# Second layer of the second block of 336 slots: 20 products over 3 x 4 tiles in the next block's steps, sums of its weights on GpSimd

## The chip, the cores and the metric

One core of one Trainium2 chip. The metric is the device time of one execution in microseconds; all numbers below are microseconds unless marked ns. The engines are TensorE (PE; PEld is its weight load), VectorE (DVE), ScalarE (ACT), GpSimd (POOL) and SyncE (SP, which only issues DMAs here).

## The reference

An RWKV-5 attention (4 batches, 8 heads, 768 tokens, 48 per head) gives 3072 tokens of D = 384. They go through a mixture of 8 experts with one expert per token:

```python
for b in range(B):
    for s in range(S):
        # e: the token's own argmax, or the token before's expert, by a gate
        h = np.maximum(x[b, s] @ w1[e], 0.0)     # 384 -> 1024
        out[b, s] = p[e] * (h @ w2[e])           # 1024 -> 384
```

Everything is float32. What follows is about the two layers `x @ w1[e]` and `h @ w2[e]` of the experts.

## The kernel before

Attention and routing take the first 107 us or so. Then the experts' tokens are worked through in ten *units*, each a number of slots of one expert: two early ones of 168, then `BLOCKS` of 448, 424, 392, 376, 336, 336, 256 and 192. Counted from 0 they are units 2 to 9; the change is about **unit 7**, the second one of 336. Its neighbours are unit 6 (336), unit 8 (256) and unit 9 (192), the last.

*First layer of units 2 to 8* (`twenty`, L1227). A product of 3 D tiles x 4 F tiles x 2 token halves is made with 20 products instead of 24, for each half `g` of F. It has 10 steps (`STEPS`), and a unit so has 20, two halves of ten. A step writes its two matmuls into one of two PSUM banks (`lanes`; steps 0 to 9 use banks 0, 1, 1, 0, 1, 1, 0, 1, 0, 1), ACT copies the bank to `snap` (L1270), DVE joins what belongs together into `hg` (L1254), ACT applies the relu in place (L1259, L1262). The factors are sums of weights (`weight_sums`, 16 DVE instructions of 128x256, L1224) and of tokens (`token_sums`, 14 instructions on the unit's half width, L1210), made while the unit before is worked on.

*Second layer* (`seven`, L1324). The first 256 slots of a unit are multiplied as pairs of 2 x 2 blocks with seven products instead of eight: four pairs, 28 matmuls of 128x192, whose factors DVE makes (`sums` L1293, `factors` L1302). What is over 256 slots (80 for a unit of 336) takes plain matmuls (`rest`, L1334: 8 of 128x384). DVE joins the seven banks (L1394), ACT scales by the gate (L1412), POOL scatters the rows to the output (L1417).

*The order.* It is written by hand. After each step of a first layer `twenty` calls `wide(i, g, s)`, which gives out a little of everything else: matmuls of the second layer by the table `BEHIND` (its first half, F tiles 0 to 3, in the own unit's steps of g = 1, its second half in the next unit's steps of g = 0), and so many DVE steps from the lists `ws`, `ts`, `fs`, `js` by the tuples in the code. These fills lie between a step's matmuls and the next ones, while ACT copies the bank. POOL gathers the tokens of the unit after the next one (L1159), each gather behind a copy of one column to `seen` (L1155), which holds it until `hg` has come so far. SP fetches weights in the order in which buffers come free (`fetch`).

*The end.* Unit 9 is done plainly in a final loop over its 8 F tiles (`hidden` L1186, then `rows` L1427 and `half_rows` L1434); unit 8's second half of the second layer lies in it by the table `LAST`. The last rows are scaled on DVE (L1444) and scattered.

Each engine works through its own queue in order.

Of the kernel before, what the change touches and what calls it, by code (L numbers as in the profile page):

```python
# [20 lines left out]
P = 128  # L21
# [1048 lines left out]
class Experts:  # L1070
# [6 lines left out]

    def __init__(self, tc, st, x_d, w1, w2, out, ident, router):
# [11 lines left out]
        self.units += [unit(None, n, b * ST, r.gid, r.sid, r.gate) for b, n in enumerate(BLOCKS)]  # L1090

        self.outs = dram_disjoint_views(out, sum(len(u["cols"]) for u in self.units))
# [121 lines left out]
    def weight_sums(self, i):  # L1214

        nc, u = self.nc, self.units[i]
        w, t = u["w1"], self.weps[i % 2].tile([P, 14, 2, P], F32, name="ws", tag="ws")
        u["ws"] = t

        def of(a):  # L1220
            return t[:, a] if isinstance(a, int) else w[:, a[0]::4, a[1]]

        def step(out, a, b, op):
            return lambda: nc.vector.tensor_tensor(t[:, out], of(a), of(b), op=Alu.add if op == "+" else Alu.subtract)  # L1224

        return [step(*s) for s in WEIGHT_SUMS]

# [6 lines left out]
    def twenty(self, i, g, then):  # L1234
# [29 lines left out]
        for s, (c, k, place) in enumerate(STEPS):  # L1264
            bank = self.lanes[min(c, 1)]
            for z, (a, b) in enumerate(CHAINS[c][k]):
                nc.tensor.matmul(bank[:, z * n:(z + 1) * n], lhsT=left(a), rhs=right(b), start=(k == 0 and z == 0),  # L1267
                                 stop=(k == len(CHAINS[c]) - 1), skip_group_check=True)
            source = bank[:, :2 * n].rearrange("p (x c) -> p x c", x=2)
            nc.scalar.copy(self.snap[:, place, :, :n], source[:, ::-1] if (c, k) in TURNED else source)  # L1270
            self.settle()
            self.owed[0].extend(join(*j) for j in JOINS.get(s, ()))
            if s in DONE:
                self.owed[1].append(lambda s=s: done(DONE[s]))
            then(s)

    def output(self, i, m, tiles=range(DK)):
# [176 lines left out]
    def send(self, i, j):  # L1454
        nc, u = self.nc, self.units[i]
        n, c = u["rows"][j], u["cols"][j]
        tp = self.bank("otp")[:, :D].rearrange("p (k t) -> p k t", k=DK)
        first = j * P - (2 * P if u["seven"] else 0)
        for d in range(DK):
            nc.tensor.transpose(tp[:n, d], u["yT"][:, d, first:first + n], self.ident)  # L1460
        yo = self.op.tile([P, D], F32, name="yo", tag="yo")
# [56 lines left out]
    def run(self, att, flag, ready, free):  # L1518
# [10 lines left out]
        self.router.powers(0)  # L1529
        behind, fs, ws, ts, js, ends = {}, [], [], [], [], []  # L1530

# [17 lines left out]
        def joined(k):  # L1549
# [16 lines left out]
        def wide(i, g, s):  # L1566
# [4 lines left out]
            early = k < EARLY  # L1571
            if s == 0:
# [3 lines left out]
            if s in (1, 2) and not early:  # L1576
                self.sums(k, 2 * z + s - 1)
            at = g * 10 + s - (6 if i == EARLY else 1)
            if (i, g, s) == (EARLY, 0, 2):
# [8 lines left out]
            elif (g, s) in ((0, 9), (1, 1), (1, 3), (1, 5), (1, 7), (1, 9)) and (i, g, s) > (EARLY, 1, 2):  # L1588
                sent()
            fill(*BEHIND[s])  # L1590
            if not u["rest"] and (g, s) in ((1, 0), (1, 1)):
                self.hidden(i + 1, s, self.tp[1])
            if g == 0:
                if s == 0 and not early:
                    fs.extend(self.factors(k, 3))
                if s == (6 if i == EARLY else 3):
# [4 lines left out]
                some(ws, (0, 0, 0, 0, 0, 0, 0, 0, 0, 2)[s] if i == EARLY else (0, 0, 0, 0, 0, 3, 4, 3, 3, 0)[s])  # L1601
                if i == EARLY and s == 4:
                    drained(k)
                    self.fetch(i + 1, self.nc.sync, 2)
                if s == 9 and not early:
                    joined(k)
# [3 lines left out]
            else:  # L1610
# [18 lines left out]
        for i in range(n):  # L1629
# [11 lines left out]

            lag = 6 if i == n - 1 else 1
            for m in range(FK):
                if following and m == FK - 1:
                    turned(i + 1, after - 1)
                if i < n - 1 or m > 1:
                    self.hidden(i, m)
                if (i, m) == (0, 0):
                    att.turn(B * HP - 1, yb[1:])
                if i == n - 1:  # L1650
                    if m in (2, 3, 4):
                        self.settle()
                    if m == 2:
                        behind = self.seven(i - 1, 1)
                        fs.extend(self.factors(i - 1, 3))
                        some(fs, 4)
                    if m in (2, 3):
                        self.sums(i - 1, m)
                    if m in LAST:
                        fill(*LAST[m])  # L1660
                    if m == 5:
                        joined(i - 1)
                        some(js, 9)
                    if m in (6, 7):
                        some(ends, 1)
                if sends and m >= 1 and i > EARLY:
                    self.send(*sends.pop(0))
                if i == n - 1:
                    if m >= lag:
                        self.rows(m - lag)  # L1670
                elif m >= lag and not (following and m > FK - 3):
                    self.output(i, m - lag)
# [6 lines left out]
                if following and m == 3:  # L1679
                    ws.extend(self.weight_sums(i + 1))  # L1680
                if following and m >= 3:
# [11 lines left out]
        for m in range(FK - lag, FK):  # L1693
            self.rows(m)
        self.send_rows(0)
        self.half_rows()
# [46 lines left out]
def kernel(  # L1743
# [41 lines left out]
    with ExitStack() as st, tc.manual_schedule():  # L1785
        ro = st.enter_context(tc.tile_pool(name="ro", bufs=1))
        mpp = st.enter_context(tc.tile_pool(name="mpp", bufs=1, space=PSUM))
        router = Router(tc, ro, mpp, lt, mask, ident, gid, sid, gate, over[:, 0:1])
        ex = Experts(tc, st, x_d, w1, w2, out, ident, router)
        att = Attention(tc, st, rk_d, kv_d, vT_d, x_d, w_t, wp_d, kept, ident, lt, router.mp)  # L1790
# [100 lines left out]
```

## Time and profile before

| | us |
|---|---|
| median of 3 runs | 367.23 (366.93 to 367.93) |
| the profiled execution | 367.12 |
| its span, first to last instruction | 365.4 |
| SP's weight fetches, 1536 KB each, w1: issue to landing | 6.7 |
| sums of tokens, 128x168 on DVE (L1210), mean | 0.326 |

A group of the profile has the line, engine and operation, the tiles written and read, the shape and the count, then its busy time and the mean ns of one, then the engine's idle time ahead of it and what ended it. In a list by time the columns are the start from the span's first instruction, the busy time, the engine, line and operation, and how many instructions lie in that row. A 128x192 matmul of float32 is two records, and a row's count counts records.

### The profile page before, as it was taken

Reading aid. Unit: us, or ns where it says so; the run is one execution under the profiler, and the core shown is the slowest. Engines: PE = TensorE matmul, PEld = TensorE weight load, DVE = VectorE, ACT = ScalarE, POOL = GpSimd, SP = SyncE. Lnnn points to the kernel's source line nnn. Section 1 sums busy time; section 2 is a strip of 40 time slices with the busy share of each in tenths; the row PEclk is TensorE's granted clock in tenths of the full one; section 3 lists DMA queues with packets and bytes.
Section 4 is the critical chain, followed back from the end, with each engine's and each line's share of the span. In section 5 each row is a group of like instructions: output and inputs, shape, how many; then the busy total and the mean of one; then the engine's idle time right before and its main releaser. Section 6 shows DMA issues by size and latency. Waiting matters only on the chain. (4 is left out here: it accounts for less than half of the span.)

```text
span 365.4 us, 9346 instructions
## 1 busy us (share of the span) xinstructions
PE 355.2 (97%) x3574; PEld 309.9 (85%) x3574; DVE 281.6 (77%) x806; ACT 158.2 (43%) x397; POOL 167.1 (46%) x212
## 2 busy tenths in 40 slices
PE   7999999999999999999999999999999999999991
PEld 4776877777769999888889999998998988899971
DVE  7888778788835768897989869879979989947530
ACT  5222232223523214845545557546555546546310
POOL 8589999789522057128174115313604114012022
PEclk9999999999999999999999999999999999999997
DMA  7999999992658766914125516416336326425011
GB/s 252 410 408 408 407 409 380 356 348 101 215 175 292 277 224 215 395 60 162 68 101 192 194 35 226 155 61 237 97 135 236 132 86 228 173 68 198 2 44 37
DMA packets 17380, 74.91 MB, mean 205 GB/s; under 512 B 2394, under 2 KB 6240, under 8 KB 15024
## 3 DMA queue, kind: packets, MB, share of 16 engines
q1 hardware_dynamic: 10336, 56.89, 41.6%
q0 software_dynamic: 3424, 9.48, 7.6%
q10 hardware_dynamic: 3568, 7.87, 5.8%
q8 instruction: 30, 0.49, 0.5%
q14 instruction: 22, 0.18, 0.2%
HBM read 64.79 MB, written 9.47 MB: 203 GB/s over the span
## 5 line engine op out<-in xcount | busy, mean ns | idle before, releaser
L1270 ACT COPY snap<-h 128x336 f32<-128x336 f32 (+5 forms) x140 | 65.0, 464 | 88.1 <-PE h L1267 83.4
L1417 POOL DMA_INDIRECT out_dram<-yo,sid x27 | 32.4, 1201 | 92.7 <-ACT yo L1412 77.1
L1159 POOL DMA_INDIRECT xg<-x_d,gid x29 | 32.8, 1131 | 28.6 <-DVE gid L926 19.3
L1267 PE MATMUL h<-xs,ws 128*128 128x168 f32 (+5 forms) x224 | 44.2, 320 | 0.0
L1254 DVE TENSOR_TENSOR hg<-snap 128x336 f32<-128x336 f32 (+5 forms) x56 | 30.0, 536 | 18.2 <-ACT snap L1270 17.8
L1267 PEld LDWEIGHTS h<-xs,ws 128*128 128x128 f32 x224 | 37.2, 190 | 5.2 <-issue 1.4
L1324 PE MATMUL y<-factors,sums 128*128 128x192 f32 x168 | 38.8, 327 | 0.0
L326 DVE TENSOR_TENSOR am<-pair,kept 128x768 f32<-128x768 f32 x32 | 29.9, 952 | 9.3 <-PE pair L316 5.7
L1155 POOL COPY seen<-hg 128x1 f32<-128x1 f32 x26 | 12.5, 480 | 52.0 <-ACT hg L1259 47.6
L240 POOL TENSOR_TENSOR pd<-rk 128x384 f32<-128x384 f32 x32 | 31.8, 1016 | 7.4 <-DMA rk<-in_rk_dram 3.9
L1324 PEld LDWEIGHTS y<-factors,sums 128*128 128x128 f32 x168 | 28.4, 190 | 0.1
L1324 PE MATMUL y<-w2t,hg 128*128 128x192 f32 x112 | 25.3, 328 | 0.0
L1334 PE MATMUL tp<-w2t,hg 128*80 128x384 f32 (+2 forms) x64 | 24.6, 487 | 0.0
L354 ACT COPY xT<-y 128x768 f32<-128x768 f32 x15 | 12.0, 798 | 29.0 <-PE y L346 29.0
L1224 DVE TENSOR_TENSOR ws<-w1t 128x256 f32<-128x256 f32 x56 | 21.9, 416 | 3.3 <-DMA w1t<-in_w_dram 3.3
L257 POOL TENSOR_TENSOR rw<-rk,tab 128x384 f32<-128x384 f32 x26 | 23.6, 932 | 0.4 <-DMA rk<-in_rk_dram 0.4
L1186 PE MATMUL h<-exT,w1t 128*128 128x168 f32 (+1 forms) x132 | 23.5, 315 | 0.0
L333 PE MATMUL y<-am,kv 128*64 128x128 f32 x360 | 23.0, 277 | 0.0
L236 POOL TENSOR_TENSOR ke<-kv,endT 128x288 f32<-128x288 f32 (+1 forms) x32 | 21.9, 706 | 0.9 <-DMA kv<-in_kv_dram 0.9
L1267 PE MATMUL h<-exT,ws 128*128 128x168 f32 (+5 forms) x112 | 22.1, 319 | 0.0
L1267 PE MATMUL h<-xs,w1t 128*128 128x168 f32 (+5 forms) x112 | 21.8, 319 | 0.0
L333 PEld LDWEIGHTS y<-am,kv 128*64 128x64 f32 x360 | 19.3, 137 | 1.9 <-issue 1.1
(296 smaller groups left out, 799.4 us busy)
## 6 DMA issues: line engine op xcount, KB each, us to landing
w1t<-in_w_dram SPq DMA_DIRECT2D x8, 1536.0 KB, 6.7
w2t<-in_w_dram SPq DMA_DIRECT2D x8, 1536.0 KB
rk<-in_rk_dram SPq DMA_DIRECT2D x15, 768.0 KB, 8.7
kv<-in_kv_dram SPq DMA_DIRECT2D x16, 584.0 KB, 8.1
vT<-in_vT_dram SPq DMA_DIRECT2D x16, 384.0 KB
x_d<-x ACTq DMA_DIRECT2D x4, 1152.0 KB
w1t<-in_w_dram SPq DMA_DIRECT2D x2, 768.0 KB
w2t<-in_w_dram SPq DMA_DIRECT2D x2, 768.0 KB
```

Source lines behind the costliest of these rows:

```text
L240: nc.gpsimd.tensor_mul(t["pd"][:, z], t["rT"][:, z], t["kT"][:, z])
L257: engine.tensor_mul(t["rw"][:, z], t["rT"][:, z], spread(pw, 1, z.stop - z.start))
L326: return lambda: nc.vector.tensor_mul(t["am"][:, g], sc, spread(kept, 1, 2))
L333: nc.tensor.matmul(t["y"][h][p * DP:(p + 1) * DP, c2 * P:(c2 + 1) * P], lhsT=t["v"][:, (2 * c + h) * DH:(2 * c + h) * DH + DP], rhs=t["am" ...
L1159: self.nc.gpsimd.indirect_dma_start(out=xg[:n], out_offset=None, in_=self.x_d[:rows], in_offset=bass.IndirectOffsetOnAxis(ap=u["gid"][:n, ...
L1186: nc.tensor.matmul(h[:, :n], lhsT=u["w1"][:, m, kk, :], rhs=u["xT"][:, kk, :], start=(kk == 0), stop=(kk == DK - 1))
L1254: return lambda: nc.vector.tensor_tensor(o, a, self.snap[:, b, :, :n], op=Alu.add if op == "+" else Alu.subtract)
L1267: nc.tensor.matmul(bank[:, z * n:(z + 1) * n], lhsT=left(a), rhs=right(b), start=(k == 0 and z == 0), stop=(k == len(CHAINS[c]) - 1), skip ...
L1270: nc.scalar.copy(self.snap[:, place, :, :n], source[:, ::-1] if (c, k) in TURNED else source)
L1324: nc.tensor.matmul(bank[:, x * half:(x + 1) * half], lhsT=a(), rhs=b(), start=first, stop=(count(k) == FK // 2), skip_group_check=True)
L1334: nc.tensor.matmul(u["y"][:z, :D], lhsT=u[m][:, 2 * P:2 * P + z], rhs=h[:, m], start=first, stop=last)
L1417: self.nc.gpsimd.indirect_dma_start(out=out.rearrange("n (h d) -> (n h) d", h=2) if half else out, out_offset=bass.IndirectOffsetOnAxis(ap ...
```

## The change

Unit 7's second layer no longer goes through `seven`. It is computed transposed, as the first layer is: 3 D tiles x 4 F tiles x 2 token halves (168 slots each) in 20 products for each half of F, 40 matmuls of 128x168 (`deeply`). They lie in unit 8's 20 steps, by the table `DEEP`. Their weight factors are 16 sums of 128x256 (`second_sums`), made on POOL; their token factors are sums of halves of `hg` on DVE (`halves`); ACT copies six banks (`keep`), DVE joins them (`side`). The result comes out transposed, so that nine transposes and three scalings follow in the final loop (`send`).

Eight of the sixteen weight sums of unit 8's first layer (`ASIDE`) go to POOL as well. Unit 6's second half of the second layer is spread over all of unit 7's 20 steps (`LONG`) and joined at the end of unit 7 instead of its middle; unit 8's second layer lies wholly in the final loop (`LAST`), as do all of unit 9's matmuls. Nothing before unit 6's second half changes.

```diff
+SECOND_SUMS = ((1, (0, 0), (0, 2), "+"), (0, (1, 1), (1, 0), "-"), (2, 0, (2, 1), "-"), (3, (2, 2), 1, "-"),
...
+DEEP = (((), ((16, 0), (17, 0)), ()),
+        (("S1",), ((16, 1), (17, 1)), ("u",)),
...
+        (("y1",), (), ()))
+LONG = (("r2",), ("1b", "r0"), ("r1",), ("1a",), ("2a", "r3"), ("6a",), ("7a",), (), ("3a",), (),
+        ("4a", "5a"), ("2b", "6b"), (), (), ("7b", "3b"), (), ("4b",), ("5b", "hr"), (), ())
+ASIDE = (10, 11, 4, 5, 12, 13, 14, 15)
...
+        if i != self.deep + 1:
+            return [step(nc.vector, *s) for s in WEIGHT_SUMS], []
+        return ([step(nc.vector, *WEIGHT_SUMS[k]) for k in range(16) if k not in ASIDE],
+                [step(nc.gpsimd, *WEIGHT_SUMS[k]) for k in ASIDE])
...
+    def second_sums(self, i, homes):
...
+            return t[a] if isinstance(a, int) else u["w2"][:, a[0]::4, a[1] * P:(a[1] + 1) * P]
+        def step(out, a, b, op):
+            return lambda: nc.gpsimd.tensor_tensor(t[out], of(a), of(b), op=Alu.add if op == "+" else Alu.subtract)
+        return [step(*s) for s in SECOND_SUMS]
...
+        def halves(k, g):
...
+                    nc.vector.tensor_tensor(out, of(a, g), of(b, g), op=add if op == "+" else sub)
+        def product(k, g):
...
+            c, z, a, b = PRODUCTS[k]
+            w = u["ss"][a][:, g] if isinstance(a, int) else u["w2"][:, 4 * g + a[0], a[1] * P:(a[1] + 1) * P]
+            nc.tensor.matmul(banks[c][:, z * n:(z + 1) * n], lhsT=w, rhs=of(b, g), start=c not in begun, stop=False,
+                             skip_group_check=True)
...
+            nc.scalar.copy(t, part(c)[:, ::-1] if k == "u" else part(c))
...
+            if deep:
+                some(ss, 1)
+                if at == 16:
+                    steps.append(self.deeply(i))
+                if at > 17:
+                    steps[0]((("S0", "V0")[at - 18:at - 17], (), ()))
+            if i == self.deep - 1 and at > 14:
+                if at == 15:
+                    ss.extend(self.second_sums(i + 1, homes))
+                some(ss, 2)
+            if done:
+                steps[0](DEEP[at])
...
+            fill(*(LONG[g * 10 + s] if deep else BEHIND[s]))
...
                 if s == 5 and following:
-                    ws.extend(self.weight_sums(i + 1))
+                    steps1, more = self.weight_sums(i + 1)
+                    ws.extend(steps1)
+                    ss.extend(more)
```

The order on POOL from unit 6's second half to the gathers of unit 9's tokens. Before, three scatters (L1417) stand in a row, two of them in unit 6's second half and the third late in unit 7's first, and behind them the gathers (L1155, L1159):

```order
L1155 COPY seen<-hg 128x1
L1159 DMA xg<-x_d,gid 128x384
L1417 DMA out_dram<-yo,sid 3072x384 x3
L1155 COPY seen<-hg 128x1
L1159 DMA xg<-x_d,gid 128x384
L1155 COPY seen<-hg 128x1
L1159 DMA xg<-x_d,gid 64x384
```

After, two scatters (L1582) are followed by eight sums (L1344, `ss`, of unit 7's second weights `w2t`), and then by these rows, in which `ws` are the sums of unit 8's first weights `w1t` (L1274):

```order
L1344 TENSOR_TENSOR ss<-w2t,ss 128x256
L1344 TENSOR_TENSOR ss<-ss,w2t 128x256
L1344 TENSOR_TENSOR ss<-w2t 128x256 x2
L1344 TENSOR_TENSOR ss<-ss 128x256 x2
L1344 TENSOR_TENSOR ss<-w2t,ss 128x256
L1582 DMA out_dram<-yo,sid 3072x384
L1344 TENSOR_TENSOR ss<-w2t,ss 128x256
L1274 TENSOR_TENSOR ws<-w1t 128x256 x2
L1274 TENSOR_TENSOR ws<-ws,w1t 128x256
L1201 COPY seen<-hg 128x1
L1205 DMA xg<-x_d,gid 128x384
L1274 TENSOR_TENSOR ws<-ws,w1t 128x256
```

The 16 sums `ss` and the first three of the eight `ws` now stand ahead of the first gather of unit 9's tokens.

The order on TensorE in unit 7's second half, from the second step on (L1320 is the first layer's line after, L1267 before; L1489 and L1324 the products of `seven`). Before, with unit 7's own products and rest (L1334) as fills:

```order
L1267 MATMUL h<-xs,ws 128x168 x2
L1324 MATMUL y_3747<-w2t,hg 128x192
L1334 MATMUL tp_1790<-w2t,hg 80x384 x2
L1267 MATMUL h<-exT,ws 128x168 x2
L1324 MATMUL y_3747<-w2t,hg 128x192 x2
L1267 MATMUL h<-xs,ws 128x168 x2
L1324 MATMUL y_3749<-factors,sums 128x192 x2
L1267 MATMUL h<-exT,ws 128x168 x2
```

After, with what is left of unit 6's second half:

```order
L1320 MATMUL h<-xs,ws 128x168 x2
L1489 MATMUL y_3503<-w2t,hg 128x192
L1489 MATMUL y_3505<-factors,sums 128x192
L1320 MATMUL h<-exT,ws 128x168 x2
L1320 MATMUL h<-xs,ws 128x168 x2
L1320 MATMUL h<-exT,ws 128x168 x2
L1489 MATMUL y_3505<-factors,sums 128x192
L1489 MATMUL mp<-w2t,sums 128x192
```

Steps 1 and 2, which use the same bank, have two products of 192 between them, and steps 2 and 4 only step 3; the plain matmuls of 384 are gone.

The order on DVE at the start of unit 8. Before, from the second join (L1254) of unit 8's first layer on, `factors` are those of unit 7's `seven`, and L1394 are its joins:

```order
L1254 TENSOR_TENSOR hg<-hg,snap 128x256
L1302 TENSOR_TENSOR factors<-factors,w2t 128x192
L1254 TENSOR_TENSOR hg<-snap 128x2x128
L1254 TENSOR_TENSOR hg<-hg,snap 128x2x128
L1254 TENSOR_TENSOR hg<-snap 128x256
L1394 TENSOR_TENSOR yo<-y_3747,t 128x192
L1394 TENSOR_TENSOR t<-y_3749,t 128x192 x2
```

After, the tile named `factors` (and `xs` further on) holds the sums of halves of unit 7's `hg` (L1385, L1387), and L1408 is a join of `deeply`:

```order
L1307 TENSOR_TENSOR hg<-snap 128x256
L1307 TENSOR_TENSOR hg<-hg,snap 128x256
L1387 TENSOR_TENSOR factors<-factors,hg 128x168 x2
L1408 TENSOR_TENSOR ws<-ws 128x336
L1387 TENSOR_TENSOR xs<-hg 128x168
L1385 SCALAR_TENSOR_TENSOR xs<-hg 128x168
L1387 TENSOR_TENSOR xs<-hg 128x168
L1385 SCALAR_TENSOR_TENSOR xs<-hg 128x168
L1307 TENSOR_TENSOR hg<-snap 128x2x128
```

What stands between unit 8's joins is no longer `seven`'s factors but sums of halves.

More of the change, by code (lines that the diff above doesn't have):

```diff
@@ L1070, with __init__ @@
 class Experts:
-    def __init__(self, tc, st, x_d, w1, w2, out, ident, router):
+    def __init__(self, tc, st, x_d, w1, w2, out, ident, router, keep):
+        self.keep = keep
         self.tc, self.nc = tc, tc.nc
@@ new lines, in aside, with deeply, pair, of @@
+    def aside(self, i):
+        u = self.units[i]
+        if "aside" not in u:
+            u["aside"] = self.weps[i % 2].tile([P, 4 * self.units[i + 1]["n"] + 6 * u["n"]], F32, name="ws", tag="ws")
+        return u["aside"]
+    def deeply(self, i):
+        nc, u = self.nc, self.units[i]
+        n, add, sub = u["n"] // 2, Alu.add, Alu.subtract
+        raw = [u["hs", g].rearrange("p f (x c) -> p (f x) c", x=2) for g in range(2)]
+        pairs, kept, banks, begun = {}, {}, [], set()
+        def pair(k):
+            if k in "SQV" and k not in pairs:
+                pairs[k] = self.sp.tile([P, 2, 2, n], F32, name="factors", tag="factors", bufs=3)
+            elif k not in pairs:
+                t = self.spare.tile([P, 3, 2, 2, n], F32, name="xs", tag="x", bufs=2)
+                for x, k2 in enumerate("RWX"):
+                    pairs[k2] = t[:, x]
+            return pairs[k]
+        def of(a, g):
+            if isinstance(a, int):
+                return raw[g][:, a]
+            if isinstance(a, str):
+                return pair(a)[:, g]
+            if isinstance(a[0], str):
+                return pair(a[0])[:, g, a[1]]
+            return raw[g][:, a[0]::a[1] - a[0]][:, :2] if a[0] < a[1] else raw[g][:, a[1]:a[0] + 1][:, ::-1]
+        def halves(k, g):
+            terms = HALVES[k]
+            for x, (a, b, op) in enumerate(terms):
+                out = raw[g][:, 3 * x] if k == "Z" else pair(k)[:, g] if len(terms) == 1 else pair(k)[:, g, x]
+                if op == "--":
+                    nc.vector.scalar_tensor_tensor(out, of(a, g), -1.0, of(b, g), Alu.mult, sub)
+                else:
+                    nc.vector.tensor_tensor(out, of(a, g), of(b, g), op=add if op == "+" else sub)
+        def product(k, g):
+            if not banks:
+                banks.extend([self.tp[1]] + [self.yps.tile([P, 512], F32, name=f"y{d}") for d in (1, 2)])
+            c, z, a, b = PRODUCTS[k]
+            w = u["ss"][a][:, g] if isinstance(a, int) else u["w2"][:, 4 * g + a[0], a[1] * P:(a[1] + 1) * P]
+            nc.tensor.matmul(banks[c][:, z * n:(z + 1) * n], lhsT=w, rhs=of(b, g), start=c not in begun, stop=False,
+                             skip_group_check=True)
+            begun.add(c)
+        def part(c, z=None):
+            t = banks[c][:, :2 * n].rearrange("p (x c) -> p x c", x=2)
+            return t if z is None else t[:, z]
+        def keep(k):
+            kept[k] = t = self.aside(i)[:, 4 * BLOCKS[i + 1 - EARLY]:].rearrange("p (k x c) -> p k x c", k=6, x=2)[:, "uakvbe".index(k)]
+            c = {"u": 0, "a": 0, "e": 0, "v": 2}.get(k, 1)
+            nc.scalar.copy(t, part(c)[:, ::-1] if k == "u" else part(c))
+        def tt(out, a, b, op):
+            nc.vector.tensor_tensor(out, a, b, op=op)
+        def side(k):
+            t = kept
+            if k == "t":
+                tt(t["u"], t["u"], t["a"], sub)
+            elif k == "add":
+                tt(part(1, 0), part(1, 0), t["v"][:, 0], add)
+                tt(part(1, 1), part(1, 1), t["v"][:, 1], sub)
+            elif k == "y2":
+                tt(t["e"][:, 1], t["b"][:, 1], t["e"][:, 1], sub)
+                tt(t["b"][:, 0], t["k"][:, 1], t["b"][:, 0], add)
+                tt(t["k"][:, 1], part(2, 0), t["e"][:, 1], add)
+                tt(t["b"][:, 1], part(2, 1), t["e"][:, 0], sub)
+            elif k == "y0":
+                tt(t["u"], part(1), t["u"], add)
+            elif k == "y1":
+                tt(t["k"][:, 0], part(0, 1), t["k"][:, 0], add)
+                tt(t["b"][:, 0], part(0, 0), t["b"][:, 0], sub)
+                u["yT"] = [t[x].rearrange("p x c -> p (x c)") for x in "ukb"]
+            else:
+                halves(k[0], int(k[1]))
+        def step(s):
+            ahead, products, after = s
+            for k in ahead:
+                side(k)
+            for k, g in products:
+                product(k, g)
+            for k in after:
+                keep(k)
+        return step
@@ L1457, in send @@
         tp = self.bank("otp")[:, :D].rearrange("p (k t) -> p k t", k=DK)
-        first = j * P - (2 * P if u["seven"] else 0)
+        first = j * P - (2 * P if u["seven"] and i != self.deep else 0)
         for d in range(DK):
-            nc.tensor.transpose(tp[:n, d], u["yT"][:, d, first:first + n], self.ident)
+            nc.tensor.transpose(tp[:n, d], (u["yT"][d] if i == self.deep else u["yT"][:, d])[:, first:first + n], self.ident)
         yo = self.op.tile([P, D], F32, name="yo", tag="yo")
@@ L1529, in run @@
         self.router.powers(0)
-        behind, fs, ws, ts, js, ends = {}, [], [], [], [], []
+        behind, fs, ws, ts, js, ends, ss = {}, [], [], [], [], [], []
+        steps, r = [], self.router
+        homes = ((r.once, "ohq0", 6), (r.once, "eqv0", 1), (r.once, "val0", 1), (self.keep, "kept", 2),
+                 *((att.late, tag, 1) for tag in ("wp", "held", "lT", "end7")))
         def fill(*names):
@@ L1604, in wide @@
                     self.fetch(i + 1, self.nc.sync, 2)
-                if s == 9 and not early:
+                if s == 9 and not early and not deep and not done:
                     joined(k)
@@ L1640, in run @@
                 continue
-            lag = 6 if i == n - 1 else 1
+            lag = 1
             for m in range(FK):
@@ L1650, in run @@
                 if i == n - 1:
-                    if m in (2, 3, 4):
+                    if m < 3:
                         self.settle()
-                    if m == 2:
-                        behind = self.seven(i - 1, 1)
-                        fs.extend(self.factors(i - 1, 3))
-                        some(fs, 4)
[L1657 to L1661, printed above, removed]
+                    z, names = LAST[m]
+                    if m == 0:
+                        sends.extend((self.deep, j) for j in range(len(self.units[self.deep]["rows"])))
+                    if m in (0, 4):
+                        behind = self.seven(i - 1, z)
+                    if m < 4:
+                        self.sums(i - 1, m)
+                        fs.extend(self.factors(i - 1, m + 1) if m < 3 else [])
+                        some(fs, 4)
+                    fill(*names)
+                    if m == 6:
                         joined(i - 1)
+                    if m == 7:
                         some(js, 9)
-                    if m in (6, 7):
-                        some(ends, 1)
                 if sends and m >= 1 and i > EARLY:
                     self.send(*sends.pop(0))
[L1668 to L1671, printed above, removed]
+                if i < n - 1 and m >= lag and not (following and m > FK - 3):
                     self.output(i, m - lag)
@@ L1692, in run @@
                 drained(i)
-        for m in range(FK - lag, FK):
+        for m in range(FK):
             self.rows(m)
+        some(ends, 9)
         self.send_rows(0)
@@ L1788 @@
         router = Router(tc, ro, mpp, lt, mask, ident, gid, sid, gate, over[:, 0:1])
-        ex = Experts(tc, st, x_d, w1, w2, out, ident, router)
+        ex = Experts(tc, st, x_d, w1, w2, out, ident, router, keep)
         att = Attention(tc, st, rk_d, kv_d, vT_d, x_d, w_t, wp_d, kept, ident, lt, router.mp)
```

86 lines of the change are left out of this document (62 added, 24 removed), and 8 rows, old and new, of tables (PRODUCTS, SECOND_SUMS).

## The prediction

> **What bounds the kernel now.** I read the page's first two parts first, then a table of stages cut at unit boundaries, then single rows of TensorE, VectorE (DVE) and GpSimd (POOL) in the last 80 us.
>
> ```profile
> span 365.4 us, 9346 instructions
> ...
> PE 355.2 (97%) x3574; PEld 309.9 (85%) x3574; DVE 281.6 (77%) x806; ACT 158.2 (43%) x397; POOL 167.1 (46%) x212
> ...
> PE   7999999999999999999999999999999999999991
> ...
> DVE  7888778788835768897989869879979989947530
> ...
> POOL 8589999789522057128174115313604114012022
> PEclk9999999999999999999999999999999999999997
> ```
>
> PE is busy in 97% of the span at full granted clock, with 9s up to the last slice: the time is the sum of what PE issues, plus any hole that the change tears. The stages (columns: length, then PE, PEld, DVE, ACT, POOL busy with counts, granted clock, DMA share, GB/s) are: unit 6's second half (from 277.01), unit 7's two halves (289.84, 303.33), unit 8's (316.16, 328.60), the final loop (339.56, 349.00) and the tail after PE's last matmul.
>
> ```profile
> 277.01:289.84 12.83, 12.83 (x79) 11.56 (x77) 12.16 (x44) 7.31 (x18) 3.42 (x4) 1.00 0.49 180
> 289.84:303.33 13.49, 13.49 (x85) 12.21 (x83) 11.97 (x38) 7.16 (x18) 2.48 (x3) 1.00 0.39 132
> 303.33:316.16 12.83, 12.83 (x79) 11.56 (x78) 12.15 (x45) 7.31 (x18) 3.37 (x4) 1.00 0.44 170
> 316.16:328.60 12.44, 12.44 (x85) 10.98 (x84) 7.29 (x24) 6.33 (x18) 0.92 (x1) 1.00 0.45 147
> 358.10:365.40 7.30, 0.00 (x0) 0.00 (x0) 0.40 (x1) 0.00 (x0) 0.97 (x1) 0.68 0.09 27
> ```
>
> PE has no hole in these stages. DVE is second: 12.16 of 12.83 us, 11.97 of 13.49 and 12.15 of 12.83 are busy, so from 277 to 316 it has about a tenth to spare. POOL looks free, 2.5 to 3.4 us of each stage, and that is the room that the change uses. From 316.16 on DVE has room too (7.29 of 12.44).
>
> **The change, part by part.** *TensorE.* A matmul of the program is two records here; its price is the distance between starts.
>
> ```profile
> 281.63 0.73 PE L1267 MATMUL h<-xs,ws 128*128 128x168 f32 x4
> 282.20 0.81 PE L1324 MATMUL y<-factors,sums 128*128 128x192 f32 x4
> 282.85 0.73 PE L1267 MATMUL h<-exT,ws 128*128 128x168 f32 x4
> ...
> 291.62 0.49 PE L1172 MATMUL tp<-ident,xg 128*128 128x128 f32 x3
> 291.95 0.49 PE L1324 MATMUL y<-w2t,hg 128*128 128x192 f32 x2
> ...
> 305.44 1.45 PE L1334 MATMUL tp<-w2t,hg 128*80 128x384 f32 x4
> 306.73 0.73 PE L1267 MATMUL h<-exT,ws 128*128 128x168 f32 x4
> ```
>
> One of 168 costs .57/2 = .285 us, one of 192 .65/2 = .325, one of 384 1.29/2 = .645, a transpose .33/3 = .11. Unit 7 loses 28 products of 192 (9.1 us) and 8 matmuls of 384 (5.16), and gets 40 of 168 (11.4) and 9 transposes (1.0): **-1.9 us** of PE. Everything else on PE (unit 6's and unit 8's products, the last unit's layers) only changes its place.
>
> *Holes between steps.* A first-layer step writes one of two banks, and ACT must copy it before the next step on that bank. Fill between them covers this; the new order leaves several pairs with too little. Nothing in the trace shows such a pair bare, so I go by one that is almost bare:
>
> ```profile
> 142.84 0.92 PE L1267 MATMUL h<-xs,ws 128*128 128x224 f32 x4
> 143.59 1.02 PE L1283 MATMUL y<-hg,w2t 128*128 128x168 f32 x6
> ...
> 143.79 0.53 ACT L1270 COPY snap<-h 128x448 f32<-128x448 f32 x1 [0.22 <-PE h L1267]
> ...
> 144.38 0.68 PEld L1267 LDWEIGHTS h<-exT,ws 128*128 128x128 f32 x4
> 144.45 0.77 PE L1267 MATMUL h<-exT,ws 128*128 128x224 f32 x3
> ...
> 303.53 0.44 ACT L1270 COPY snap<-h 128x336 f32<-128x336 f32 x1 [0.73 <-PE h L1267]
> L1270 ACT COPY snap<-h 128x256 f32<-128x256 f32 x11 | 4.1, 372 | 6.1 <-PE h L1267 6.0
> ```
>
> The last h matmul is issued ahead of 143.59, the copy starts at 143.79 and lasts .53, the next weight load starts .06 after its end and the matmul (144.45) .07 after that: .86 us from bank to bank. A 336-wide copy takes .44 instead of .53, one of 256 .37: .8 and .7 us. In the new order six pairs have less between them: in unit 7's second half twice two products of 192 (.65), once the step between (.57), once, into unit 8, a whole step (.57); in unit 8's second half twice two products of 168 (.57). Open are .15 twice, .23 twice and .13 twice: 1.0 us; .4 I add for unit 8's first half, where ACT's new copies stand ahead of the bank's. The ends are 0 (PE's sequencer runs ahead and nothing opens) and 2.5 (another .25 at each of the six); I take **+1.4**. So far 367.1 - 1.9 + 1.4 = 366.6.
>
> *VectorE and GpSimd.* DVE loses unit 7's sums and factors (32), 7 joins and 8 weight sums, and gets 22 half sums and 10 joins: it has less to do. POOL gets 24 sums of 128x256 that stand nearly in one row in its queue (one scatter and two gathers are among the last nine): from the two scatters in unit 6's second half, of which the last runs from 283.83 to 284.91, so with the .3 between POOL's neighbours from about 285.2. No row shows that size on POOL; the neighbours do:
>
> ```profile
> 283.83 1.08 POOL L1417 DMA_INDIRECT out_dram<-yo,sid  x1 [0.30 <-issue]
> ...
> L236 POOL TENSOR_TENSOR ke<-kv,endT 128x288 f32<-128x288 f32 x17 | 13.6, 802 | 0.9 <-DMA kv<-in_kv_dram 0.9
> ...
> L161 POOL TENSOR_TENSOR tab<-tab 128x384 f32<-128x384 f32 x1 | 0.8, 831 | 0.1
> L161 POOL TENSOR_TENSOR tab<-tab 128x192 f32<-128x192 f32 x1 | 0.5, 509 | 0.1
> ```
>
> Between 509 and 831 lies .62; the 288-wide mean of 802 less a ninth is .71. I take .64: 24 sums are **15.4 us** on POOL.
>
> The question is what a POOL sum costs DVE. These rows (POOL, then DVE, place by place) say that the two shut each other out when DVE reads two SBUF operands:
>
> ```profile
> 278.79 0.18 POOL L1155 COPY seen<-hg 128x1 f32<-128x1 f32 x1 [2.27 <-ACT hg L1259]
> 278.18 0.74 DVE L1394 TENSOR_TENSOR t<-y,t 128x192 f32<-128x192 f32 x2
> ...
> 301.14 0.47 POOL L1155 COPY seen<-hg 128x1 f32<-128x1 f32 x1
> 300.39 0.51 DVE L1254 TENSOR_TENSOR hg<-snap 128x336 f32<-128x336 f32 x1 [0.50 <-ACT snap L1270]
> 300.82 0.42 DVE L1224 TENSOR_TENSOR ws<-w1t 128x256 f32<-128x256 f32 x1
> 301.15 0.42 DVE L1224 TENSOR_TENSOR ws<-w1t,ws 128x256 f32<-128x256 f32 x1
> ...
> 184.26 2.62 POOL L1155 COPY seen<-hg 128x1 f32<-128x1 f32 x1
> ...
> 69.69 1.96 POOL L257 TENSOR_TENSOR rw<-rk,tab 128x384 f32<-128x384 f32 x2
> 70.80 0.88 DVE L750 SCALAR_TENSOR_TENSOR key<-lt,k 128x12 f32<-128x12 f32 x1
> ...
> L750 DVE SCALAR_TENSOR_TENSOR key<-lt,k x2: 174/528/882, 70.8 to 111.5; 128x12 f32<-128x12 f32 x2
> ```
>
> POOL's copy of one column takes .18 us beside L1394, which reads PSUM; beside L1224, which reads SBUF twice, it takes .47 and ends .04 after that instruction's end (301.57); at 184.26 it takes 2.62. The other way round, DVE's 12-column L750 takes 882 ns instead of 174, ending (71.68) just behind POOL's two sums (69.69 + 1.96 = 71.65). So I count POOL's sums and DVE's two-SBUF work as one queue.
>
> What that queue must pass between 285.2 and the end of unit 7: that end would be 316.16 less unit 7's own fills that leave its steps (half of its 9.1 + 5.16, that is 7.1) plus .65 of the holes, 309.7, so there are **24.5 us**. DVE needs 4.4 of the 4.6 us to 289.84 (it is as full there as the stage row says). After that, in unit 7, stand 16 instructions of 336 columns, 8 of 256, 5 of 192 and 22 of 128. By starts, 300.39 to 300.82 gives .43, 300.82 to 301.15 .33; 192 and 128 columns by the same line (.10 per 80 columns) .26 and .19. That is 6.9 + 2.6 + 1.3 + 4.2 = 15.0. With POOL's 15.4 the queue holds 34.8 us in a window of 24.5: **10.3 us too much**. PE waits for nearly all of it: the joins (L1254) free `snap`, ACT's copy waits for them, and PE's bank waits for the copy; unit 8's first steps wait for token sums and weight sums. Two 336-wide halves at the end (.86) are not wanted at once, so 9.5 is what I let through. Below nothing it can't go, as no sum gets shorter; without any lock it is 0; the upper end is a rival.
>
> [...]
>
> The sum: 367.1 - 1.9 + 1.4 + 9.5 = 376.1 for an execution like the profiled one (367.12: span 365.4 and 1.7 around it), which lies .1 under the median of 367.23: **376.2 us**.
>
> The tail (7.30 us) keeps its last links (DVE's last scaling, a scatter); unit 8's joins come ahead of some 8 us of the last unit's matmuls, which hide them, and I cost that at nothing (about 2 us if the scatters queue).
>
> **The rivals.**
> 1. *Hidden: the sums run beside DVE.* The place is POOL's streak from 285 to 301; it decides this way if DVE's joins keep their .43 there. For it: long DVE work does pass beside POOL in the first 107 us, with one operand in PSUM:
>
> ```profile
> L326 DVE TENSOR_TENSOR am<-pair,kept 128x768 f32<-128x768 f32 x32 | 29.9, 952 | 9.3 <-PE pair L316 5.7 <-PE pair L323 3.4
> ```
>
> Against it: L750's 882. It gives 366.6 + .1 = 366.7, no change; if the fills also cover the holes, 367.2 - 1.9 = 365.3, faster.
> 2. *POOL starves.* As at 184.26, a closed row of DVE work keeps POOL out. The gather of unit 9's tokens stands behind 19 sums in POOL's queue, and PE transposes these tokens in unit 8's second step. If the sums get in only when DVE runs dry (309.7), the gather starts at 309.7 + 19 x .64 = 321.9 and takes a microsecond, wanted at about 310.6, and the new products wait for their factors in the same way: some 12 to 17 us, 379 to 384.
> 3. *The clock falls.* A hole of several us lets the granted clock drop: the tail's row shows .68 where PE does nothing. If it stayed at that for 3 us after the largest hole, 1 us is added: 377.2. [...]
> 4. *The change doesn't do what it says* (scatters keep POOL's sums back, so they start late in unit 7): a part of the lock then falls into unit 8, where DVE has 5 us to spare: 3 to 5 us instead of 9.5, about 371.
>
> **How the numbers follow.** The lock as summed, with or without the clock's microsecond (372 to 379): .53. Starved (379 to 386): .14. Partly hidden (368.4 to 372): .07. Hidden with the holes: .14. Hidden without them: .12. I forecast 376.2. The range goes from 366.2, which takes in the hidden case, to 384.0; outside lie most of the fast case and a part of the starved one. No change is within 0.3% of 367.23 (366.1 to 368.3), about what a measurement of this kernel can tell: slower .74, same .14, faster .12.
>
> **What would show it.** PE's sum: 40 matmuls at the new line with .285 between starts, PE busy near 353.3. The lock: POOL's sums well over .64 us each and DVE's L1254 and L1224 lines with means well over .5 and .42 between 285 and 315, and holes of PE there that end with ACT's copies. If DVE's means stay and POOL's sums are near .64, the forecast is wrong and 366.7 stands. If the largest hole of PE ends with a gather's landing, rival 2 is right; if the clock's row shows less than 9 behind a hole, rival 3 adds its part. Holes of .3 to .6 us between steps with nothing on DVE beside them are the bank turnaround.

## The result and the profile after

| | before | after |
|---|---|---|
| median | 367.12 (366.93 to 367.93, 4 runs) | 377.77 (376.60 to 379.32, 4 runs) |
| ratio | | 1.0296 (95% interval 1.0271 to 1.0322) |
| span of the profiled execution | 365.4 | 376.7 |

The changed kernel is slower by 3.0%, about 10.7 us; its profiled execution (378.35) lies .6 above its median, so the spans differ by 11.3. All ratios compare fast executions; one of the ten with fills of zero (below) took 919.71 us in a slow state and is not in its ratio. The page after:

```profile
span 376.7 us, 9396 instructions
...
PE 358.5 (95%) x3591; PEld 312.5 (83%) x3591; DVE 292.5 (78%) x791; ACT 160.4 (43%) x402; POOL 186.8 (50%) x236
...
PE   7999999999999999999999999999999497999992
...
POOL 8789999789511164255553036046039538100322
PEclk9999999999999999999999999999999799999998
```

A slice is 9.4 us long. In the one from 292 us PE stands at 4 and its clock at 7; POOL stands at 9 in the slice ahead of it. PE's busy time rose by 3.3 us although it has 1.9 us less to issue: the same work is busy for longer at a lower clock (four records of a 168-column step last 1.28 us from start to start at a clock of .50, .57 at 1.00), and small delays between matmuls count as busy (in the run with fills of zero below, PE reads 10.60 us busy of 10.60 from 300.00 to 310.60, although the four records at 304.33 last .68 and not .57). DVE's rose by 10.9 although it has 15 instructions fewer. A table of stages (columns as in the prediction's table: length, PE, PEld, DVE, ACT, POOL, granted clock, DMA share, GB/s), cut at the holes:

```profile
277.01:289.84 12.83, 12.40 (x73) 10.83 (x72) 12.15 (x29) 6.69 (x18) 8.30 (x11) 1.00 0.46 172
289.84:296.90 7.06, 2.03 (x13) 1.37 (x11) 7.06 (x10) 0.91 (x3) 7.06 (x9) 0.95 0.61 224
296.90:303.20 6.30, 6.30 (x18) 4.62 (x19) 5.72 (x21) 2.75 (x8) 0.00 (x0) 0.52 0.00 0
303.20:313.00 9.80, 9.14 (x60) 8.53 (x58) 8.47 (x16) 5.55 (x13) 5.84 (x7) 1.00 0.04 13
313.00:323.00 10.00, 8.32 (x52) 7.37 (x52) 9.73 (x21) 5.72 (x17) 5.47 (x8) 1.00 0.64 214
323.00:334.00 11.00, 11.00 (x86) 10.61 (x85) 9.22 (x31) 7.88 (x23) 2.04 (x2) 1.00 0.41 156
```

The kernel before from 289.84 to 296.90:

```profile
289.84:296.90 7.06, 7.06 (x44) 6.09 (x43) 6.08 (x21) 4.14 (x11) 0.00 (x0) 1.00 0.56 212
```

From 289.84 to 296.90 PE does 2.03 us of work, while DVE and POOL are both "busy" for the whole 7.06 us, DVE with 10 instructions where it did 21 in that time before. Then PE runs 6.30 us at a mean clock of .52. From 323 on no hole in TensorE is over .2 us. The rows of DVE and POOL at the start of it:

```profile
284.45 2.23 DVE L1307 TENSOR_TENSOR hg<-snap 128x336 f32<-128x336 f32 x1
286.72 0.92 DVE L1307 TENSOR_TENSOR hg<-hg,snap 128x336 f32<-128x336 f32 x1
287.56 1.62 DVE L1260 TENSOR_TENSOR xs<-exT 128x168 f32<-128x168 f32 x2
289.11 0.86 DVE L1260 TENSOR_TENSOR xs<-xs,exT 128x168 f32<-128x168 f32 x1
289.88 0.85 DVE L1260 TENSOR_TENSOR xs<-exT,xs 128x168 f32<-128x168 f32 x1
...
304.46 0.51 DVE L1307 TENSOR_TENSOR hg<-snap 128x336 f32<-128x336 f32 x1 [1.74 <-ACT snap L1323]
...
316.35 2.72 DVE L1307 TENSOR_TENSOR hg<-hg,snap 128x336 f32<-128x336 f32 x1
...
284.89 1.42 POOL L1344 TENSOR_TENSOR ss<-w2t 128x256 f32<-128x256 f32 x2
286.39 0.88 POOL L1344 TENSOR_TENSOR ss<-ss,w2t 128x256 f32<-128x256 f32 x1
287.23 0.99 POOL L1344 TENSOR_TENSOR ss<-w2t,ss 128x256 f32<-128x256 f32 x1
288.18 3.14 POOL L1344 TENSOR_TENSOR ss<-w2t 128x256 f32<-128x256 f32 x4
...
306.97 1.15 POOL L1582 DMA_INDIRECT out_dram<-yo,sid  x1 [10.07 <-ACT yo L1577]
...
316.60 0.73 POOL L1274 TENSOR_TENSOR ws<-ws 128x256 f32<-128x256 f32 x1
317.29 1.40 POOL L1274 TENSOR_TENSOR ws<-w1t 128x256 f32<-128x256 f32 x2
```

The same join and token sums in the kernel before:

```profile
284.50 0.50 DVE L1254 TENSOR_TENSOR hg<-snap 128x336 f32<-128x336 f32 x1
...
285.94 0.33 DVE L1210 TENSOR_TENSOR xs<-xs,exT 128x168 f32<-128x168 f32 x1
286.19 0.33 DVE L1210 TENSOR_TENSOR xs<-exT,xs 128x168 f32<-128x168 f32 x1
286.43 0.57 DVE L1210 TENSOR_TENSOR xs<-exT 128x168 f32<-128x168 f32 x2
```

From 288 on both queues run in lockstep, one instruction of each in turn: a token sum starts every .77 us (289.11, 289.88) where before one started every .245, and a POOL sum every .78 (four in 3.14). In lockstep each POOL sum costs DVE .77 - .245 = .53 us. Twice POOL got more than its turn: two sums ran while DVE's join, .50 us before, took 2.23 (284.45), and three while one took 2.72 (316.35). These sums don't depend on each other, but neither do the four at 288.18, which took turns; what makes the difference no run shows. The wait passes on as predicted; ACT's and PE's rows behind it:

```profile
296.40 0.78 ACT L1323 COPY snap<-h 128x336 f32<-128x336 f32 x2 [6.15 <-DVE hg L1307]
...
296.90 1.49 PE L1320 MATMUL h<-xs,ws 128*128 128x168 f32 x4 [5.03 <-ACT snap L1323]
298.18 0.85 PE L1218 MATMUL tp<-ident,xg 128*128 128x128 f32 x3
...
303.15 0.73 PE L1320 MATMUL h<-xs,ws 128*128 128x168 f32 x4
...
313.27 0.84 PE L1320 MATMUL h<-exT,ws 128*128 128x168 f32 x4 [0.93 <-ACT snap L1323]
...
320.03 0.84 PE L1320 MATMUL h<-xs,w1t 128*128 128x168 f32 x4 [1.40 <-ACT snap L1323]
```

DVE's join at 295.29 stands behind ten of the unit's twelve token sums (the trace has twelve to a unit, not the fourteen of the description above), each of them slowed; ACT's copy waits 6.15 us for it, and PE's bank 5.03 us for the copy. After that four records of a 168-column step take 1.28 us (296.90 to 298.18); four such records take .57 at 303.15.

### The profile page after: what moved, and what is told of

The parts are those of the page before. It is cut to its first block, busy times and chain, and to the rows that moved or that the text cites. A ratio compares the mean times of both kernels' runs of the same rounds, so it can differ in the third digit from the quotient of the medians.

```text
span 376.7 us, 9396 instructions
## 1 busy us (share of the span) xinstructions
PE 358.5 (95%) x3591; PEld 312.5 (83%) x3591; DVE 292.5 (78%) x791; ACT 160.4 (43%) x402; POOL 186.8 (50%) x236
## 5 line engine op out<-in xcount | busy, mean ns | idle before, releaser
L1582 POOL DMA_INDIRECT out_dram<-yo,sid x27 | 32.4, 1198 | 87.4 <-ACT yo L1577 42.7
L1320 PE MATMUL h<-xs,ws 128*128 128x168 f32 (+5 forms) x224 | 45.0, 324 | 5.0 <-ACT snap L1323 5.0
L1320 PEld LDWEIGHTS h<-xs,ws 128*128 128x128 f32 x224 | 37.4, 193 | 9.6 <-ACT snap L1323 5.7
L1307 DVE TENSOR_TENSOR hg<-snap 128x336 f32<-128x336 f32 (+5 forms) x52 | 31.6, 609 | 14.4 <-ACT snap L1323 14.0
L1489 PE MATMUL y<-factors,sums 128*128 128x192 f32 x144 | 33.3, 327 | 0.0
L1232 PE MATMUL h<-exT,w1t 128*128 128x168 f32 (+1 forms) x144 | 25.8, 316 | 0.0
L1489 PEld LDWEIGHTS y<-factors,sums 128*128 128x128 f32 x144 | 24.5, 190 | 0.1
L1320 PE MATMUL h<-exT,ws 128*128 128x168 f32 (+5 forms) x112 | 23.1, 330 | 0.9 <-ACT snap L1323 0.9
L1320 PE MATMUL h<-xs,w1t 128*128 128x168 f32 (+5 forms) x112 | 21.9, 321 | 1.8 <-ACT snap L1323 1.8
L1274 DVE TENSOR_TENSOR ws<-w1t 128x256 f32<-128x256 f32 x52 | 20.4, 419 | 2.8 <-DMA w1t<-in_w_dram 2.8
L1232 PEld LDWEIGHTS h<-exT,w1t 128*128 128x128 f32 x144 | 21.9, 190 | 0.3 <-issue 0.2
L1312 ACT ACTIVATE hg<-hg 128x336 f32<-128x336 f32 (+5 forms) x39 | 19.0, 516 | 7.2 <-DVE hg L1307 7.2
L1320 PEld LDWEIGHTS h<-exT,ws 128*128 128x128 f32 x112 | 18.8, 195 | 3.8 <-ACT snap L1323 2.0
```

What stands on the lines that cost most here:

```text
L1232: nc.tensor.matmul(h[:, :n], lhsT=u["w1"][:, m, kk, :], rhs=u["xT"][:, kk, :], start=(kk == 0), stop=(kk == DK - 1))
L1307: return lambda: nc.vector.tensor_tensor(o, a, self.snap[:, b, :, :n], op=Alu.add if op == "+" else Alu.subtract)
L1489: nc.tensor.matmul(bank[:, x * half:(x + 1) * half], lhsT=a(), rhs=b(), start=first, stop=(count(k) == FK // 2), skip_group_check=True)
L1582: self.nc.gpsimd.indirect_dma_start(out=out.rearrange("n (h d) -> (n h) d", h=2) if half else out, out_offset=bass.IndirectOffsetOnAxis(ap ...
```

## The experiments

The theory: GpSimd's sums and VectorE's instructions with two SBUF operands shut each other out, as the lockstep above shows it (.77 us from one token sum to the next in place of .245). The expectations call it the port theory; that a port is the cause no run shows. Rival A: the holes come from TensorE's new order. Rival B: the sums' results are late, wherever they are made.

**All sums on VectorE, in the same places.**

```diff
-            return lambda: nc.gpsimd.tensor_tensor(t[out], of(a), of(b), op=Alu.add if op == "+" else Alu.subtract)
+            return lambda: nc.vector.tensor_tensor(t[out], of(a), of(b), op=Alu.add if op == "+" else Alu.subtract)
...
-                [step(nc.gpsimd, *WEIGHT_SUMS[k]) for k in ASIDE])
+                [step(nc.vector, *WEIGHT_SUMS[k]) for k in ASIDE])
```

> The same program with all 24 sums issued on VectorE instead of GpSimd, in the same places of the program; TensorE's order is untouched. Port theory (GpSimd's sums and VectorE's two-SBUF instructions shut each other out): the 24 sums cost VectorE 24 x .335 = 8.0 us instead of 15.4 or more in the common queue, so the queue of 24.5 us holds 19.6 + 8.0 = 27.6, 3 us too much; the time falls to 369 to 371. Rival A (the holes come from TensorE's new order: banks turned round too soon): nothing changes, 376 to 379. Rival B (the sums are simply late, on whichever engine): VectorE finishes them later still, behind its joins, and the time rises over 379.

Measured: 370.9 (ratio 1.0097, 1.0070 to 1.0124). The same work, on the engine that is already the second fullest, and 6.9 us are gone. What is left is VectorE's overload; stages and PE's largest hole:

```profile
289.84:301.00 11.16, 9.34 (x54) 7.45 (x54) 11.02 (x37) 6.02 (x15) 0.01 (x1) 1.00 0.39 142
301.00:314.00 13.00, 11.89 (x76) 10.90 (x75) 11.98 (x38) 7.49 (x20) 7.27 (x5) 1.00 0.27 86
...
294.49 0.87 PE L1499 MATMUL tp<-w2t,hg 128*80 128x384 f32 x2 [1.33 <-ACT hg L1312]
```

DVE is full (11.02 of 11.16 us) with 37 instructions, and the clock stays at 1.00. Rivals A and B fall as causes of the large hole.

**The kernel before, with 24 idle sums on GpSimd** (the sixteen second-layer sums, the first eight of them twice).

```diff
+            if i == n - 3:
+                some(ss, 1)
+            if i == n - 4 and at > 14:
+                if at == 15:
+                    ss.extend(self.second_sums(i + 1, homes))
+                    ss.extend(ss[:8])
+                some(ss, 2)
```

> The kernel before, and nothing of the change but 24 sums of 128x256 on GpSimd at the same places, written to tiles that nothing reads. Port theory: the common queue from 285 to the end of unit 7 (316.2) holds GpSimd's 24 x .8 = 19 us as now measured beside VectorE, or 24 x .64 = 15.4 alone, and VectorE's two-SBUF work of about 25 us; 40 to 44 us in a window of 31: 9 to 13 us more, 376 to 380, although nothing waits for the sums. Rival A (TensorE's order): 367.2, as nothing of that order changes. Rival B (the sums' results are late): 367.2 too, as nobody reads them; only the two gathers behind them could come late.

Measured: 380.04 (ratio 1.0328, 1.0259 to 1.0398). This is the upper end of what was expected. Sums that nobody reads cost the kernel before about as much as the whole change does (the two ratios' intervals overlap). Its stages:

```profile
290.00:297.96 7.96, 2.93 (x18) 2.27 (x16) 7.96 (x11) 0.93 (x3) 7.96 (x12) 0.96 0.54 199
297.96:304.24 6.28, 5.86 (x15) 3.86 (x16) 6.18 (x21) 2.31 (x7) 0.80 (x2) 0.51 0.00 0
304.24:315.50 11.26, 11.26 (x73) 10.56 (x71) 9.42 (x20) 5.34 (x13) 4.61 (x7) 1.00 0.25 77
315.50:318.21 2.71, 0.17 (x3) 0.00 (x1) 2.71 (x6) 0.29 (x1) 1.68 (x2) 0.92 0.86 354
318.21:321.40 3.19, 3.19 (x7) 1.85 (x8) 3.09 (x10) 1.47 (x5) 2.17 (x4) 0.53 0.15 45
```

It is the same hole at the same place, and the same 6.3 us at .51 behind it; a second hole of 2.7 us also brings the clock down, for 3.2 us.

**Fills with zero in place of the sums.**

```diff
-            return lambda: nc.gpsimd.tensor_tensor(t[out], of(a), of(b), op=Alu.add if op == "+" else Alu.subtract)
+            return lambda: nc.gpsimd.memset(t[out], 0.0)
```

(the eight first-layer sums likewise).

> The changed kernel with GpSimd's 24 sums replaced by 24 fills with zero of the same tiles: the weight sums are left out, GpSimd writes SBUF but reads none of it. Port theory, if the lock is taken for reading: no hole from it, the time is 367.2 less 1.9 plus the bank turnaround of about 1.4: 366.7 (365.5 to 367.5). If writing takes the lock as well: fills of .4 to .6 us in the common queue, 371 to 376. Rival A (TensorE's order): 376 to 379, since that order is untouched.

Measured: 367.5 (ratio 0.9997, 0.9968 to 1.0027). VectorE and GpSimd now overlap freely:

```profile
286.01 3.14 POOL L1346 MEMSET ss<- 128x256 f32 x12
...
287.07 0.33 DVE L1260 TENSOR_TENSOR xs<-xs,exT 128x168 f32<-128x168 f32 x1
287.31 0.33 DVE L1260 TENSOR_TENSOR xs<-exT,xs 128x168 f32<-128x168 f32 x1
287.56 0.57 DVE L1260 TENSOR_TENSOR xs<-exT 128x168 f32<-128x168 f32 x2
```

Twelve fills in 3.14 us, and beside them DVE's token sums start every .245 us as in the kernel before. So what shuts DVE out is not that GpSimd is busy, nor that it writes; what a sum does beyond a fill of the same size is to read SBUF and to add. The one-column copies of the kernel before, which VectorE kept out for up to 2.62 us, read SBUF and add nothing. The run also shows the rest of the change by itself: TensorE's starts show holes of 1.7 us in all from 304 to 329, at the pairs of steps that the prediction names and in unit 8's first steps, so that -1.9 + 1.7 is left.

**Only the second layer's sums on GpSimd** (the eight of unit 8's first layer back on VectorE, one word in the last line of the first diff).

> The changed kernel with the eight first-layer sums of unit 8 back on VectorE and the sixteen second-layer sums still on GpSimd. Port theory: GpSimd brings 16 x .64 = 10.2 us instead of 15.4 to the queue, VectorE 2.7 us more: 32.4 instead of 34.8 us, so 2.4 us less: about 375. The largest hole (5.2 us at 297) stays as it is, since it comes from the first fifteen sums. Rival A: 377.8. If only the first fifteen sums matter: 376 to 377.

Measured: 376.27 (ratio 1.0256, 1.0170 to 1.0341), 1.5 less than the change's median and 1.3 more than the 375 expected; it lies in the 376 to 377 of the case in which only the first fifteen sums matter. The interval takes in the changed kernel's ratio, so the times alone don't tell the two apart; the trace does. Its large hole is unchanged (5.2 us); what went is the hole of 1.6 us at 320 and a quarter of the one at 313. So the first fifteen sums make most of the loss.

**The sums on VectorE by need.** As in the first run, and given out by step: `EACH` has the steps of unit 7 with one second-layer sum each, `AFTER` those of unit 8 for the other six, `APART` those for six first-layer sums.

```diff
+EACH = (0, 1, 2, 3, 4, 10, 12, 14, 16, 18)
+AFTER = {1: 2, 3: 2, 10: 1, 12: 1}
+APART = {0: 2, 2: 2, 4: 2}
+ASIDE = (10, 11, 12, 13, 14, 15)
...
+                if at in EACH:
+                    some(ss, 1)
...
+                some(ss, AFTER.get(at, 0))
+                some(late, APART.get(at, 0))
```

> All 24 sums on VectorE, and spread by need: ten of the second-layer sums and two of the first-layer ones in unit 7's steps, six and six in unit 8's. Port theory: no port is shared any more, and VectorE has 32.2 us from unit 7 to the middle of unit 8 in which it was 25.6 busy without the sums; 22 sums there are 7.4 us, .8 too much. TensorE's holes of the bank turnaround (1.7) stay. So 367.1 - 1.9 + 1.7 + .8 = 367.7 (367 to 369), and no hole over 1 us at 297 or 307. Rival B (the sums are late wherever they run): 371 or more, as ten of them come later in the program than they did with all on VectorE at the old places.

Measured: 368.35 (ratio 1.0030, 1.0017 to 1.0044). Nothing is left at 297, and no more than the turnaround at 307; one hole of 1.2 us came at 315, where unit 8's new products wait for half sums on VectorE.

**The same, and the fills moved.**

```diff
-LONG = (("r2",), ("1b", "r0"), ("r1",), ("1a",), ("2a", "r3"), ("6a",), ("7a",), (), ("3a",), (),
-        ("4a", "5a"), ("2b", "6b"), (), (), ("7b", "3b"), (), ("4b",), ("5b", "hr"), (), ())
+LONG = ((), ("1b", "r0"), ("r1",), (), ("2a", "r3"), ("6a",), ("7a",), (), ("3a",), (),
+        ("5a",), ("2b", "6b", "4b"), ("r2",), (), ("7b", "3b", "4a"), (), (), ("5b", "hr"), ("1a",), ())
```

and in `DEEP` the product (3, 1) one step later and (8, 1) one step later.

> The run before, and the fills between the first layer's steps moved so that no two steps on one bank stand with less than .85 us between them: in unit 7 five of unit 6's matmuls go from its first to its second half, in unit 8 two products by one step. If the holes of .04 to .18 us at each pair are the bank turnaround, about 1.0 of the 1.7 us goes: 366.7 (366 to 368). If they are something else on ACT or VectorE, nothing changes against the run before.

Measured: 368.06 (ratio 1.0020, 1.0007 to 1.0033): a miss, .3 less in place of 1.0, within the two runs' spread. The holes at the named pairs went. Two of .12 opened at 291 and 308, at pairs that gave their fills away (they are in the next run too), and one of .23 at 303 that the next run, with less on VectorE, doesn't have; the hole at 315 stayed:

```profile
314.83 0.50 DVE L1390 TENSOR_TENSOR factors<-factors,hg 128x336 f32<-128x336 f32 x1
...
315.38 0.84 PE L1397 MATMUL tp<-factors,ss 128*128 128x168 f32 x4 [0.96 <-DVE factors L1390]
```

**The fills with zero, and the moved fills.**

> The fills of zero in place of the sums again (the weight sums are left out), with the moved fills of the run before. It shows the bank turnaround by itself: 367.5 of that run less 1.0 gives 366.5 (366.0 to 367.0), TensorE's holes from unit 7 on .7 in place of 1.7. If the holes belong to something else: 367.5 again.

Measured: 366.14 (ratio 0.9982, 0.9963 to 1.0001). By the ratios that is .7 us under the kernel before, where the fills with zero alone were .1 under it, but the two intervals overlap; TensorE's holes went from 1.7 to 1.1 where .7 was expected. So by the trace the bank turnaround that these fills remove is .6 us, not 1.0.

**Rebalanced.** All sums on VectorE with the moved fills, and none ahead of the half sums in unit 8's first steps:

```diff
-EACH = (0, 1, 2, 3, 4, 10, 12, 14, 16, 18)
-AFTER = {1: 2, 3: 2, 10: 1, 12: 1}
-APART = {0: 2, 2: 2, 4: 2}
-ASIDE = (10, 11, 12, 13, 14, 15)
+EACH = (0, 2, 4, 10, 12, 13, 14, 15, 16, 17)
+AFTER = {4: 2, 5: 2, 10: 1, 12: 1}
+APART = {3: 2, 7: 2}
+ASIDE = (12, 13, 14, 15)
```

> All sums on VectorE and the moved fills, with the sums shifted so that none stands ahead of the half sums that unit 8's first steps wait for: unit 7 makes ten second-layer and twelve first-layer sums, more of them in its second half, unit 8 six and four from its fourth step on. The run before lost 1.2 us of TensorE in one hole at 315 behind VectorE's half sums; without it 368.06 - 1.2 = 366.9, and down to 366.1 if VectorE's queue has no other late place (the time with the sums left out). If VectorE has too little room altogether, the hole turns up elsewhere and the time stays at 368.

Measured: 367.22 against 367.87 for the kernel before, run beside it (ratio 0.9984, 0.9964 to 1.0003), where 366.9 was expected. The hole at 315 is gone, but the one at 303 grew from .23 to .40 us, so VectorE's queue did have another late place. The median is 2.8% under the changed kernel's; against the kernel before the interval reaches over 1, so a gain is not shown.

## Why the prediction was right, and where its sizes were off

The sign and the place were right: the rows of one-column copies that grew from .18 to .47 us, and of the 12-column instruction that took 882 ns, did stand for two engines that shut each other out, and the forecast put the loss at 9.0 us where 10.7 came. That the total came so near is in part luck: the clock's 3.0 us were left out of the sum, and the queue's term is right by errors that nearly cancel. By its steps, the measured ones from TensorE's starts in the changed kernel:

| step | predicted | measured |
|---|---|---|
| TensorE's own work | -1.9 | -1.9 (17 records more, 3591 for 3574, as the counts give, at the prediction's prices) |
| bank turnaround | +1.4 | +1.7 (fills with zero in place of the sums) |
| the common queue | +9.5 | +8.6 (.7 at 288, 5.2 at 297, .1 at 299, 1.0 at 313, 1.6 at 320; .15 of the one at 313 counts as turnaround) |
| the clock | 0 (rival 3: 1.0) | +3.0 (the matmuls from 296.9 to 303.2 at .52) |
| sum | +9.0 | +11.4, span +11.3 |

*The common queue* was right in kind and nearly in size, by errors that offset each other. In lockstep a sum costs VectorE .53 us and not .64; that alone would take 2.6 us from the term. The 22 instructions of 128 columns were 20 (twelve token sums), .4 us less. On the other side, five of the sums ran two and three in a row, and cost 1.7 and 2.2 us instead of 1.1 and 1.6. And the sum lets the queue use all of its window, but the last nine sums didn't come in the row: a scatter (306.97, after 10.07 us of waiting for ACT) held them to 308 and later, and meanwhile VectorE stood idle for 1.74 us (up to 304.46). How much of each reached TensorE no run tells apart. The late nine are rival 4's case in part only: they ran from 308 to 318.7, still in unit 7 and not in unit 8's spare time, and cost about 2.7 us in the holes at 313 and 320, since VectorE was full in that stage too (9.73 of 10.00 us).

*The clock* was the mis-sized term. Rival 3 took the tail's mean of .68 for 3 us, 1.0 us, a length that was the author's estimate and that no row had shown; the rows show .52 for 6.30 us, 3.0 us. Here are the changed kernel's stages, cut where the granted clock changes and every 3.41 us:

```profile
292.75:296.16 3.41, 0.00 (x0) 0.00 (x0) 3.41 (x5) 0.00 (x0) 3.41 (x6) 1.00 0.55 227
296.16:299.57 3.41, 2.67 (x10) 2.24 (x10) 3.41 (x10) 1.34 (x4) 0.74 (x1) 0.50 0.00 0
299.57:302.99 3.42, 3.42 (x9) 2.33 (x9) 3.05 (x13) 1.91 (x6) 0.00 (x0) 0.50 0.00 0
302.99:306.40 3.41, 3.41 (x22) 2.94 (x22) 1.87 (x5) 1.54 (x4) 0.00 (x0) 1.00 0.00 0
...
316.64:320.05 3.41, 2.01 (x15) 1.72 (x13) 3.28 (x6) 1.33 (x4) 2.05 (x3) 1.00 0.87 295
```

And those of the run with idle sums at its second hole:

```profile
314.36:317.77 3.41, 1.30 (x7) 0.74 (x5) 3.41 (x6) 0.62 (x2) 2.79 (x3) 1.00 0.93 379
317.77:321.18 3.41, 2.97 (x6) 1.76 (x7) 3.31 (x11) 1.77 (x5) 1.96 (x4) 0.50 0.16 56
```

The clock was half from 296.16 to 302.99, that is 6.83 us, and in the other run from 317.77 to 321.18, 3.41 us: two stretches of 3.41 us and one. It fell behind a stretch with 0.00 and behind one with 1.30 us of TensorE's work, and not behind one with 2.01; it came back behind 3.42 and 2.97 us of work, and not behind 2.67. What sets the clock between these values no run shows.

*How they take turns.* From 288 on the two engines took turns, .77 us for a pair. The two long joins didn't: by their rows they started ahead of GpSimd's sums (284.45 against 284.89, 316.35 against 316.60) and still waited for two and for three of them, 2.23 and 2.72 us in all. The other way round, VectorE kept a copy out for 2.62 us in the kernel before (184.26), while its own rows lay one behind the other from 183.40 to 187.58. What decides who goes next no run shows. GpSimd's fills with zero kept nothing out (.245 us from one token sum to the next). Rival 2 (GpSimd starved, its gathers late) didn't happen: the gathers ran at 312.47 and 315.50, and no hole of TensorE ends with one. Rival 1's time, 366.7, is near what came when fills stood in place of the sums (367.5, and 366.1 with better fills).

*What the change could give.* The 1.9 us that TensorE saves are real, but the bank turnaround takes 1.1 to 1.7 back, and the 24 sums need some 8 us of VectorE in a stretch from unit 7 to the middle of unit 8 that had 6.6 to spare (32.2 less 25.6). The best version with all its sums made is not told apart from the kernel before.

## What to carry to other kernels

GpSimd read 46% busy on the page before and still was not free: 24 sums that nobody reads made 380.04 us of 367.10. Before work goes to GpSimd, look at what VectorE does in the same microseconds, and count GpSimd's sums and VectorE's two-SBUF-operand work as one queue (in lockstep a sum cost VectorE .53 us here, a fill of the same size nothing). The cheap test is to add the work to the old kernel with nobody reading it. Holes of 5.2 us (the changed kernel) and 2.7 us (the run with idle sums) in TensorE cost 3.0 and 1.5 us more through the clock; behind those of 1.1 to 1.6 us the clock stayed at 1.00.

## What the runs showed of the hardware that was not expected

- GpSimd's fills of 128x256 take .26 us from start to start and cost VectorE nothing (.245 us from one token sum to the next, as before); sums of the same size take .77 in lockstep.
- Twice in the changed kernel a VectorE join that had started first by its row waited for more than one GpSimd sum: for two (2.23 us in all) and for three (2.72 us).
- The granted clock fell to half in holes of 5.2 and of 2.7 us and stayed there for 6.83 and 3.41 us, two stretches of 3.41 us and one; in holes of 1.1 to 1.6 us it didn't fall.
